# Windowed attention and FFN in one stream: softmax sums and PSUM copies from VectorE to ScalarE, six raw pairs for eight, a later weight decode

## The chip, the cores and the metric

The kernel runs on one core of one Trainium2 chip. The core has five engines that matter here: TensorE (PE, matmuls; its weight loads are listed as PEld), VectorE (DVE), ScalarE (ACT), GpSimd (POOL), and SyncE (SP), which only issues DMAs. Each works through its own list of instructions in order and waits on semaphores of the others. The metric is the device time of one execution in microseconds (us), the median of several runs.

## The reference

Attention over 8 batches and 8 heads of width 64, with 512 local tokens and 32 global ones, and then a two-layer FFN over all 4352 tokens that come out of it.

```python
s_g = scale * np.matmul(q_g, k_all.transpose(0, 1, 3, 2))      # global queries see everything
out_g = np.matmul(sm(s_g), v_all)
mask = np.abs(pos[:, None] - pos[None, :]) <= window            # window = 32
s_ll = np.where(mask, s_ll, -1000000000.0)                      # local queries see a band ...
s_l = np.concatenate([s_lg, s_ll], axis=-1)                     # ... and the 32 global keys
out_l = np.matmul(sm(s_l), np.concatenate([v_g, v_l], axis=2))
...
h = x @ w_in                                                    # x: 4352 x 512, w_in: 512 x 2048
g = np.maximum(h, 0.0) + alpha * np.minimum(h, 0.0)
return (g @ w_out).astype(np.float32)
```

`sm` is a softmax whose sum has 1e-9 added before the division.

## The kernel before

**Units.** The main loop counts units u. FFN unit t = u - 19 is one block of 128 hidden columns (of 16) for one group of tokens: `f1(t)` does twelve 128x512 matmuls into the PSUM tile `h_ps` (three for each of four input blocks, since x and the weights are split into a high and a low part), then VectorE makes `g` from it in two steps (L404, L405), ScalarE rounds it to `gh` (L407) and GpSimd takes the rest, `gl` (L408). `f2(t)` does twelve matmuls from `gh` and `gl` into four output banks, two units later (`LAG`). There are nine groups: one of 512 tokens for each batch, and one of the 256 global tokens. Units 0 to 18 (`NPRE` = 19) have attention alone.

**Attention.** A pair P is two heads of one batch; there are 32, four to a batch and so to a group. Pair P is worked on in units 4P to 4P+3 and finishes in the next two or three. In each unit a score block is made (`local_scores`, two row blocks of 128 queries): matmuls into `s_ps`, on VectorE one custom step for each row block that adds the mask, scales and finds the extreme (L243), on ScalarE the exponential with its row sum z (L247). Then `softmax_tail`: VectorE adds 1e-9 to the two sums one by one (L208) and takes the reciprocal (L209), ScalarE multiplies the rows (L214). The probabilities are transposed into `pt_sb` and multiplied with v into `o_ps`.

**Raw pairs and others.** The first `NRAW` pairs take q and k as they are in float32 (`qk_raw`, loaded whole by `load_pair`). Their probabilities are transposed on TensorE into PSUM (`transpose_pe`, `global_transposes`), copied to `pt_sb` by the engines that the strings `PEC` and `PEG` name for the pair's two heads ("a" ScalarE, "d" VectorE; L302 and L304), and in part by VectorE's 32-wide transposes (L318, L291). The other pairs have q and k rounded by ScalarE and split by GpSimd (`prep_qk`, tiles `hi` and `kl`, L189, L192, L195), and their probabilities go through one large VectorE transpose (L324) and a DRAM scratch, the global ones through 16 small VectorE transposes (L297).

**Weights.** 32 pieces (f, j), 512 KB each, come as 64-bit words (tile `wraw`) and are decoded once: two ScalarE steps (L112, L113), three VectorE steps, which are a clamp (L114), a shift (L116) and a merge (L117), a GpSimd addition (L119); a unit later ScalarE rounds (L125) and GpSimd takes the rest (L126). `weights_step(u)` runs at the end of each unit; `RATE` gives the pieces for units before and from 19, and each piece's load is issued six pieces ahead. Six loads are issued ahead of the loop. `f1(t)` needs piece 2t, `f2(t)` piece 2t+1.

**Order.** A scheduler orders each engine's list from priorities and a model of durations; `boost` gives attention a higher priority. From unit `PIN` on, TensorE's list keeps the program's order. In units below `NWARM` = 18, `WARM` = (2, 2) adds two matmuls of zeros ahead of the attention work and two behind it.

**Group change.** `split_x` rounds a finished batch's attention output to `xh` (ScalarE, L386) and takes the rest as `xl` (VectorE, L387), four blocks for a group, in the unit ahead of the group's first.

Of the kernel before, what the change touches and what calls it, by code (L numbers as in the profile page):

```python
# [8 lines left out]
F32 = mybir.dt.float32  # L9
# [3 lines left out]
AF = mybir.ActivationFunctionType  # L13
ALU = mybir.AluOpType
# [6 lines left out]
NC = DM // 128  # L21
NQ, NK = 512, 640
NEG = -8.0e9
NKR = 704
PEC = "ad"
PEG = "da"
NWARM = 18
WARM = (2, 2)
NRAW = 8
NWB = 33  # L30
NST = 18
NNP = [(0, 0), (0, 2)]
# [27 lines left out]
def longformer_ffn(ctx: ExitStack, tc: tile.TileContext, qk, qkr, gn, vt, vx, w, alpha, out):  # L60
    nc = tc.nc
# [35 lines left out]
    def stage(name, dtype=F32):  # L97
        return work.tile([128, 512], dtype, tag="st", name=name, bufs=NST)
# [23 lines left out]
    def split_weights(f, j):  # L122
        t = wmid.pop((f, j))
        wt = wpool.tile([128, 2, 512], F32R, tag="w", name="wt")
        nc.scalar.copy(wt[:, 0, :], t)  # L125
        nc.gpsimd.tensor_tensor(wt[:, 1, :], t, wt[:, 0, :].bitcast(F32), op=ALU.subtract)  # L126
        wts[f, j] = wt
# [41 lines left out]
    def load_v(P):  # L169
# [27 lines left out]
    def s_bank(P, kind):  # L197
        tag = BT[kind] if P < NPAIR else "s"
        return psum.tile([128, 512], F32, tag=tag, name=kind + "_ps", bufs=2 if tag in "hs" else 1)

    def small(name, n=2):
        return work.tile([128, n], F32, tag=name, name=name, bufs=3)

    def softmax_tail(ranges, z, n, pool=False):
        parts = 128
        rz = small("rz")
        for e in range(n):
            nc.vector.tensor_scalar(rz[:parts, e : e + 1], z[:parts, e : e + 1], 1e-9, None, op0=ALU.add)  # L208
        nc.vector.reciprocal(rz[:parts, 0:n], rz[:parts, 0:n])  # L209
        for e, r in enumerate(ranges):  # L210
            if pool:
                nc.gpsimd.tensor_scalar(r, r, rz[:parts, e : e + 1], 1.0, op0=ALU.mult, op1=ALU.mult)
            else:
                nc.scalar.activation(r, r, AF.Copy, scale=rz[:parts, e : e + 1])  # L214

    def local_scores(P, h, a, pool=False):
# [4 lines left out]
        for e in range(2):  # L221
            i = 2 * a + e
            if P < NRAW:
                n, c0 = 160, 0
# [6 lines left out]
            else:  # L231
# [4 lines left out]
                masks.append(mask[:, c0 : c0 + n])  # L236
            if P < NRAW:
                ranges.append(p_sb[:, base : base + n])
            else:
                ranges.append(sub_ap(p_sb, 0, 128, 896 * h + 4 * c0 + 32 * i, ((128, n // 32), (1, 32))))  # L240
        for e, pr in enumerate(ranges):
# [4 lines left out]
            )  # L246
            nc.scalar.activation(pr, pr, AF.Exp, bias=mn[:, e : e + 1], scale=-1.0, accum_out=z[:, e : e + 1])  # L247
# [34 lines left out]
    def global_transposes(P):  # L282
        if P < NRAW:
            ps = pt_bank(P, 2).rearrange("p (e q) -> p e q", e=4)
            for e in range(2):
                nc.tensor.transpose(ps[:, e, :], sg_sb[:, 128 * e : 128 * e + 128], ident)
            for h in range(2):
                copy(PEG[h], sub_ap(pt_sb, 0, 128, h * 1280 + 64, ((320, 2), (640, 2), (1, 32))), sub_ap(ps, 0, 128, 32 * h, ((128, 2), (64, 2), (1, 32))))
        for h in range(2):
            if P < NRAW:  # L290
                nc.vector.transpose(pt_sb[32:64, h, 3, 1, 64:96], sg_sb[32 * h : 32 * h + 32, 256:288])  # L291
                continue
            for a in range(2):
                for j in range(4):
                    src = sub_ap(sg_sb, 64 * a + 32 * h, 32, 32 * j, ((128, 2), (1, 32)))
                    dst = sub_ap(pt_sb, 32 * j, 32, 640 * h + 512 + a * 64, ((32, 2), (1, 32)))
                    nc.vector.transpose(dst, src)  # L297
            nc.vector.transpose(sub_ap(pt_sb, 32, 32, 1280 + 640 * h + 512 + 96, ((1, 32),)), sg_sb[32 * h : 32 * h + 32, 256:288])

    def copy(engine, dst, src):  # L300
        if engine == "a":
            nc.scalar.copy(dst, src)  # L302
        else:
            nc.vector.tensor_copy(dst, src)  # L304
# [76 lines left out]
    def split_x(G, c):  # L381
        kind, b = GROUPS[G]
        n = SL if kind == "l" else NB * SG
        src = (x_raw if kind == "l" else x_glb)[:, c, 0:n]
        xh, xl = stage("xh", F32R), stage("xl", F32R)
        nc.scalar.copy(xh[:, 0:n], src)  # L386
        nc.vector.tensor_tensor(xl[:, 0:n], src, xh[:, 0:n].bitcast(F32), op=ALU.subtract)  # L387
# [50 lines left out]
    def live(P):  # L438
        return 0 <= P < NPR
# [89 lines left out]
    pieces = [(f, j) for f in range(NF) for j in range(2)]  # L529
    ahead = 6  # L530
    state = [0]

    def weights_step(u):
        k = state[0]
        n = RATE[0][u % len(RATE[0])] if u < NPRE else RATE[1][u % len(RATE[1])]
        new = [i for i in range(k, min(k + n, len(pieces)))]
        for i in new:
            if i + ahead < len(pieces):
                load_weights(*pieces[i + ahead])
            decode_words(*pieces[i])  # L540
# [9 lines left out]
        return tc.high_priority(offset=HP) if u >= HPU else nullcontext()  # L550

    load_pair(0)
    for k in range(ahead):
        load_weights(*pieces[k])
    NT = len(GROUPS) * NF
    for t in range(-NPRE, NT + LAG):
        u = t + NPRE
        pinned[0] = u >= PIN
        if u < NWARM:
# [3 lines left out]
        G, f = divmod(t + 1, NF)  # L563
# [93 lines left out]
```

## Time and profile before

| | us |
|---|---|
| median of 3 timed runs (1019.73 to 1021.2) | 1019.75 |
| the profiled execution | 1017.19 |
| its span, first to last instruction | 1015.4 |

| engine busy over the span | us | share |
|---|---|---|
| TensorE | 984.7 | 97% |
| VectorE | 659.9 | 65% |
| ScalarE | 507.4 | 50% |
| GpSimd | 407.7 | 40% |

The profile is of one execution. Its page gives totals by engine, then the span in 40 equal slices with one digit for each slice (9 is 90% busy or more). A group row has line, engine, operation, out<-in with shapes, xcount, then busy us, mean ns of one, and idle us before it with what ended that wait. A timeline row has start, length, engine, line, operation and in brackets the idle time before it. Busy time counts overlapped instructions of an engine once, so that a busy sum is a little less than count times mean. TensorE's weight loads run beside its matmuls.

### The profile page before, as it was taken

How to read it: one execution, taken by the hardware profiler on the slowest of the kernel's cores; microseconds unless marked ns; L12 is line 12 of the kernel's file. 1: busy time of each engine (PE TensorE's matmuls, PEld its weight loads, DVE VectorE, ACT ScalarE, POOL GpSimd, SP SyncE). 2: the span in 40 equal slices, each digit the busy share in tenths (PEclk: the TensorE clock that was granted, in tenths of full speed). 3: DMA queues.
4: the chain of work that ended last, by engine and by line, in shares of the span. 5: the costliest groups of instructions: out<-in, count | busy, mean ns of one | idle time of the engine just before them, and what ended most of it. 6: DMA issues, size and time to landing. Idle time of an engine off the chain costs nothing.

```text
span 1015.4 us, 17227 instructions
## 1 busy us (share of the span) xinstructions
PE 984.7 (97%) x5592; PEld 790.2 (78%) x5592; DVE 659.9 (65%) x2274; ACT 507.4 (50%) x1347; POOL 407.7 (40%) x330
## 2 busy tenths in 40 slices
PE   7798989998999999999999999999999999999998
PEld 4455767776888888888888888888888888888798
DVE  8978778776666766676767666766667665322322
ACT  6667566575445555455446555654555542211121
POOL 7611567653344344334344344433443432222222
PEclk9987999999999999999999999999999999999999
DMA  9545432145444554455455554455455532100010
GB/s 349 224 141 176 140 116 68 60 123 185 147 138 133 177 158 137 141 167 169 135 152 158 171 153 143 144 179 157 118 149 178 159 107 79 42 1 1 1 43 22
DMA packets 95275, 133.01 MB, mean 131 GB/s; under 512 B 10192, under 2 KB 53712, under 8 KB 95184
## 3 DMA queue, kind: packets, MB, share of 16 engines
q1 hardware_dynamic: 95184, 131.91, 41.5%
q8 instruction: 44, 0.72, 0.3%
q14 instruction: 47, 0.39, 0.1%
HBM read 100.93 MB, written 30.93 MB: 130 GB/s over the span
## 4 chain that ended last, share of the span: by engine, by line
PE 84%; DVE 9%; ACT 2%; issue 2%; DMA 1%; POOL 0%; SPq 0%; DVEq 0%; ACTq 0%; POOLq 0%
PE o L92 35%; PE h_ps L92 35%; PE o_ps L92 5%; PE s_ps L92 5%; PE g_ps L92 3%; DVE wt L114 1%; DVE wt L117 1%; DVE pt_sb L318 1%; DVE p_sb L243 1%; PE warm L92 1%; ACT p_sb L214 1%; DVE g L404 1%; DVE wt L116 1%; DVE g L405 1%; ACT p_sb L247 0%
## 5 line engine op out<-in xcount | busy, mean ns | idle before, releaser
L92 PE MATMUL h_ps<-xh,wt 128*128 128x512 f32 (+1 forms) x1152 | 351.8, 389 | 2.8 <-DVE g L405 2.8
L408 POOL TENSOR_TENSOR gl<-g,gh 128x512 fp32r<-128x512 f32 (+1 forms) x144 | 177.5, 1233 | 418.1 <-ACT gh L407 382.6
L92 PE MATMUL o<-gh,wt 128*128 128x512 f32 (+1 forms) x1152 | 282.5, 386 | 1.5 <-ACT ost L302 1.5
L92 PEld LDWEIGHTS o<-gh,wt 128*128 128x128 f32 x1152 | 205.8, 188 | 48.5 <-ACT ost L302 2.5
L92 PEld LDWEIGHTS h_ps<-xh,wt 128*128 128x128 f32 x1152 | 207.4, 191 | 43.4 <-DVE g L405 3.3
L92 PE MATMUL h_ps<-xl,wt 128*128 128x512 f32 (+1 forms) x576 | 222.4, 387 | 0.9 <-DVE xl L387 0.9
L407 ACT CAST gh<-g 128x512 fp32r<-128x512 f32 (+1 forms) x144 | 86.1, 598 | 260.9 <-DVE g L405 241.4
L404 DVE TENSOR_SCALAR g<-h_ps,alpha_sb 128x512 f32<-128x512 f32 (+1 forms) x144 | 103.3, 717 | 125.3 <-PE h_ps L92 123.0
L214 ACT ACTIVATE p_sb<-p_sb,rz 128x192 f32<-128x192 f32 (+1 forms) x252 | 102.3, 454 | 118.1 <-DVE rz L209 115.8
L92 PE MATMUL o<-gl,wt 128*128 128x512 f32 (+1 forms) x576 | 151.4, 383 | 0.0
L247 ACT ACTIVATE p_sb<-p_sb,mn 128x224 f32<-128x224 f32 (+2 forms) x256 | 115.8, 454 | 39.5 <-DVE mn L243 39.3
L92 PEld LDWEIGHTS h_ps<-xl,wt 128*128 128x128 f32 x576 | 109.4, 190 | 25.2 <-DVE xl L387 1.1
L92 PEld LDWEIGHTS o<-gl,wt 128*128 128x128 f32 x576 | 104.5, 188 | 23.9 <-issue 0.8
L208 DVE TENSOR_SCALAR rz<-z 128x1 f32<-128x1 f32 x256 | 38.3, 151 | 97.4 <-ACT p_sb L247 96.0
L297 DVE STREAM_TRANSPOSE pt_sb<-sg_sb 32x64 f32<-32x64 f32 x384 | 90.6, 236 | 10.6 <-ACT sg_sb L280 4.9
L192 POOL TENSOR_TENSOR hi<-rawq,hi 64x512 fp32r<-64x512 f32 x48 | 62.1, 1294 | 88.0 <-DMA vt<-in_vt_dram 50.1
L405 DVE SCALAR_TENSOR_TENSOR g<-h_ps,g 128x512 f32<-128x512 f32 (+1 forms) x144 | 94.1, 653 | 2.8
L195 POOL TENSOR_TENSOR kl<-rawk,hi 128x640 fp32r<-128x640 f32 x48 | 75.9, 1582 | 3.8
L119 POOL TENSOR_TENSOR wt<-wt,wr 128x512 int32<-128x512 int32 x32 | 42.4, 1324 | 77.2 <-DVE rz L208 40.2
L243 DVE CUSTOM_DVE_ANT_0 p_sb<-s_ps,mask 128x192 f32<-128x192 f32 x192 | 64.3, 364 | 13.5 <-PE s_ps L92 11.9
L92 PE MATMUL o_ps<-pt_sb,vt 128*64 128x160 f32 (+4 forms) x832 | 68.2, 288 | 3.6 <-ACT pt_sb L302 1.7
L92 PEld LDWEIGHTS o_ps<-pt_sb,vt 128*64 128x64 f32 (+2 forms) x832 | 48.7, 135 | 21.9 <-issue 11.9
(85 smaller groups left out, 1043.7 us busy)
## 6 DMA issues: line engine op xcount, KB each, us to landing
scratch<-p_sb SPq DMA_DIRECT2D x192, 112.0 KB, 2.4
wraw<-in_w_dram SPq DMA_DIRECT2D x32, 512.0 KB, 6.7
vt<-in_vt_dram SPq DMA_DIRECT2D x32, 512.0 KB, 4.9
rawk<-in_qk_dram SPq DMA_DIRECT2D x96, 160.0 KB, 2.9
rawq<-in_qk_dram SPq DMA_DIRECT2D x96, 128.0 KB, 2.7
pt_sb<-scratch SPq DMA_DIRECT2D x48, 256.0 KB, 2.8
gn<-in_gn_dram SPq DMA_DIRECT2D x32, 304.0 KB, 5.3
pt_sb<-scratch SPq DMA_DIRECT2D x48, 192.0 KB, 2.9
```

The costliest lines, as they stand in the source:

```text
L92: ins = nc.tensor.matmul(*a, **k)
L119: nc.gpsimd.tensor_tensor(ti, ti, r, op=ALU.add)
L192: nc.gpsimd.tensor_tensor(q, raw[64:128], q.bitcast(F32), op=ALU.subtract)
L195: nc.gpsimd.tensor_tensor(kl[P, h], raw, t.bitcast(F32), op=ALU.subtract)
L214: nc.scalar.activation(r, r, AF.Copy, scale=rz[:parts, e : e + 1])
L243: nc.vector.tensor_tensor_reduce(out=pr, in0=s[:, 256 * e : 256 * e + nn], in1=masks[e], scale=-0.125, scalar=3.0e38, op0=ALU.add, op1=ALU ...
L247: nc.scalar.activation(pr, pr, AF.Exp, bias=mn[:, e : e + 1], scale=-1.0, accum_out=z[:, e : e + 1])
L297: nc.vector.transpose(dst, src)
L404: nc.vector.tensor_scalar(g[:, 0:n], h[:, 0:n], 0.0, alpha_sb[:, f : f + 1], op0=ALU.min, op1=ALU.mult)
L405: nc.vector.scalar_tensor_tensor(g[:, 0:n], h[:, 0:n], 0.0, g[:, 0:n], op0=ALU.max, op1=ALU.add)
L407: nc.scalar.copy(gh[:, 0:n], g[:, 0:n])
L408: nc.gpsimd.tensor_tensor(gl[:, 0:n], g[:, 0:n], gh[:, 0:n].bitcast(F32), op=ALU.subtract)
```

## The change

The edits: the sum z + 1e-9 becomes one ScalarE instruction for both sums; `PEC` and `PEG` name ScalarE alone; `NRAW` is 6 for 8; for group 0 three of the four `xl` go to GpSimd; the first six weight loads are issued one in each of units 0 to 5, inside `weights_step`; no piece is decoded before unit 3 (`WFIRST`), then one in every second unit up to unit 18, then two in each unit; `PIN` is 28 for 36. `NWARM` and `WARM` stay as they are. Lines below line 29 or so move by one or two.

```diff
-PEC = "ad"
-PEG = "da"
+PEC = "aa"
+PEG = "aa"
 NWARM = 18
 WARM = (2, 2)
-NRAW = 8
+NRAW = 6
...
-PIN = 36
+PIN = 28
...
-RATE = ((1, 1, 0), (2, 1))
+WFIRST = 3
+RATE = ((0, 1), (2,))
...
         rz = small("rz")
-        for e in range(n):
-            nc.vector.tensor_scalar(rz[:parts, e : e + 1], z[:parts, e : e + 1], 1e-9, None, op0=ALU.add)
+        nc.scalar.activation(rz[:parts, 0:n], z[:parts, 0:n], AF.Copy, bias=1e-9)
         nc.vector.reciprocal(rz[:parts, 0:n], rz[:parts, 0:n])
...
         nc.scalar.copy(xh[:, 0:n], src)
-        nc.vector.tensor_tensor(xl[:, 0:n], src, xh[:, 0:n].bitcast(F32), op=ALU.subtract)
+        eng = nc.gpsimd if G == 0 and c < NC - 1 else nc.vector
+        eng.tensor_tensor(xl[:, 0:n], src, xh[:, 0:n].bitcast(F32), op=ALU.subtract)
         xs[G, c] = (xh, xl)
...
     def weights_step(u):
+        if u < ahead:
+            load_weights(*pieces[u])
         k = state[0]
         n = RATE[0][u % len(RATE[0])] if u < NPRE else RATE[1][u % len(RATE[1])]
+        n = n if u >= WFIRST else 0
...
     load_pair(0)
-    for k in range(ahead):
-        load_weights(*pieces[k])
     NT = len(GROUPS) * NF
```

The scheduler makes new lists of it. ScalarE's list begins before with four decode steps of two pieces, then the first exponentials:

```order
L112 ACT_TABLE_LOAD
L112 ACTIVATE wt<-wraw 128x512
L113 ACTIVATE wr<-wraw 128x512
L112 ACTIVATE wt<-wraw 128x512
L113 ACTIVATE wr<-wraw 128x512
L247 ACTIVATE p_sb,z<-p_sb,mn 128x160 x4
L112 ACTIVATE wt<-wraw 128x512
L113 ACTIVATE wr<-wraw 128x512
```

Now the same place reads so:

```order
L247 ACT_TABLE_LOAD
L247 ACTIVATE p_sb,z<-p_sb,mn 128x160 x4
L208 ACTIVATE rz<-z 128x2
L113 ACTIVATE wt<-wraw 128x512
L114 ACTIVATE wr<-wraw 128x512
L208 ACTIVATE rz<-z 128x2
L113 ACTIVATE wt<-wraw 128x512
L114 ACTIVATE wr<-wraw 128x512
```

The exponentials (L247) stand first, the new sums (L208) are among them, and the first decode steps, now L113 and L114, come behind.

The second place is VectorE's list between the last steps of FFN units 8 and 9, before:

```order
L243 ISA p_sb,mn<-s_ps,rmask 128x160
L243 ISA mn 128x1
L243 ISA p_sb,mn<-s_ps,rmask 128x160
L243 ISA mn 128x1
L114 TENSOR_SCALAR wt<-wt 128x512
L208 TENSOR_SCALAR rz<-z 128x1
L116 TENSOR_SCALAR wt<-wt 128x512
L208 TENSOR_SCALAR rz<-z 128x1
L404 TENSOR_SCALAR g<-h_ps,alpha_sb 128x512
L117 SCALAR_TENSOR_TENSOR wt<-wraw,wt 128x512
L209 RECIPROCAL rz<-rz 128x2
L405 SCALAR_TENSOR_TENSOR g<-h_ps,g 128x512
```

And now, up to the same step (L406 there), behind the small transposes of the pair before:

```order
L243 ISA p_sb,mn<-s_ps,mask 128x6x32
L243 ISA mn 128x1
L115 TENSOR_SCALAR wt<-wt 128x512
L117 TENSOR_SCALAR wt<-wt 128x512
L115 TENSOR_SCALAR wt<-wt 128x512
L118 SCALAR_TENSOR_TENSOR wt<-wraw,wt 128x512
L117 TENSOR_SCALAR wt<-wt 128x512
L118 SCALAR_TENSOR_TENSOR wt<-wraw,wt 128x512
L405 TENSOR_SCALAR g<-h_ps,alpha_sb 128x512
L209 RECIPROCAL rz<-rz 128x2
L406 SCALAR_TENSOR_TENSOR g<-h_ps,g 128x512
```

Two pieces stand ahead of the unit's g for one, the two sums are gone, and the scores are those of a pair that is not raw (`mask` for `rmask`).

The third place is TensorE's list inside FFN unit 16, the first of group 1, before (pair 7, raw, finishes amid the unit's matmuls):

```order
L92 MATMUL h_ps<-xh,wt 128x512 x2
L92 MATMUL o_ps<-pt_sb,vt 64x96 x2
L92 MATMUL o_ps<-pt_sb,vx 64x64 x2
L92 MATMUL o_ps<-pt_sb,vt 64x2x64 x2
L92 MATMUL o_ps<-pt_sb,vt 64x96 x2
L92 MATMUL o_ps<-pt_sb,vx 64x64 x2
L92 MATMUL o_ps<-pt_sb,vt 64x2x64 x2
L92 MATMUL h_ps<-xl,wt 128x512
```

And now the unit and the scores ahead of it:

```order
L93 MATMUL s_ps<-hi 128x224
L93 MATMUL s_ps<-kl,hi 128x224
L93 MATMUL s_ps<-hi 128x192
L93 MATMUL s_ps<-kl,hi 128x192
L93 MATMUL h_ps<-xh,wt 128x512 x2
L93 MATMUL h_ps<-xl,wt 128x512
```

The unit's twelve matmuls now follow one another, as in all later units of both lists; this holds from FFN unit 9 on, and before from unit 18 on. From the last matmul of FFN unit 20 on, TensorE's list is the same in both.

## The prediction

> **What bounds the kernel now.** I read the page's totals and slices first, then a table of windows, then single rows. In the totals TensorE (PE) is busy 97% of the span; no other engine is above 65%.
>
> ```profile
> PE 984.7 (97%) x5592; PEld 790.2 (78%) x5592; DVE 659.9 (65%) x2274; ACT 507.4 (50%) x1347; POOL 407.7 (40%) x330
> PE   7798989998999999999999999999999999999998
> DVE  8978778776666766676767666766667665322322
> ```
>
> The average hides two regimes. In the first ten slices (254 us) VectorE (DVE) is at 6 to 9 tenths; behind them TensorE is full. To cut the trace into stretches I use VectorE's last step of FFN unit t, called g(t): g(0), g(12), g(20) are these three instructions.
>
> ```profile
> 96.74 0.69 DVE L405 SCALAR_TENSOR_TENSOR g<-h_ps,g 128x512 f32<-128x512 f32 x1
> 196.26 0.67 DVE L405 SCALAR_TENSOR_TENSOR g<-h_ps,g 128x512 f32<-128x512 f32 x1
> 259.95 0.65 DVE L405 SCALAR_TENSOR_TENSOR g<-h_ps,g 128x512 f32<-128x512 f32 x1
> 0.00:97.40 97.40, 81.11 (x536) 50.94 (x536) 79.51 (x306) 67.34 (x196) 43.41 (x50) 0.91 0.63 227
> 97.40:196.90 99.50, 95.14 (x547) 71.00 (x548) 78.85 (x208) 61.35 (x147) 63.92 (x50) 0.94 0.30 102
> 196.90:260.60 63.70, 58.86 (x334) 46.58 (x333) 45.82 (x167) 37.24 (x98) 28.43 (x23) 0.97 0.44 134
> 260.60:1015.40 754.80, 749.63 (x4178) 621.70 (x4176) 455.73 (x1599) 341.50 (x906) 271.92 (x208) 1.00 0.41 122
> ```
>
> The last four rows give window, length, then busy time (instructions) of PE, its weight loads, DVE, ACT, POOL, then granted clock, DMA share, GB/s. In the **prelude**, to g(0), TensorE's 81 us hold 72 warming matmuls; the busiest engine with work to do is VectorE, 79.5/97.4 = 82%. In the **ramp**, g(0) to g(12), TensorE is busy 96% at clock 0.94, VectorE 79%. In the **settling** stretch, g(12) to g(20), eight units take 63.7 us. The last 754.8 us are TensorE at 99%, in a rhythm:
>
> ```profile
> 274.68 2.13 PE L92 MATMUL o<-gh,wt 128*128 128x512 f32 x8
> 301.67 2.13 PE L92 MATMUL o<-gh,wt 128*128 128x512 f32 x8
> ```
>
> Those two rows are the same place of two successive pairs: 27.0 us for four units, 6.75 a unit.
>
> **The end: no change.** In the order, TensorE's 3776 instructions from the last matmul of unit 20 on are the same before and after. TensorE is busy there 749.6 of 754.8 us, so VectorE's and ScalarE's edits lie beneath it; cover lost would show only if VectorE, now 456 of 755, became the slower one. I keep 754.8. The whole question is when g(20) comes: 260.6 now.
>
> **Prelude.** The order puts g(0) behind the same attention work in both (42 score blocks, 5.25 pairs) but less else.
>
> ```profile
> L117 DVE SCALAR_TENSOR_TENSOR wt<-wraw,wt 128x512 uint32<-128x512 uint32 x13 | 12.5, 964 | 0.1
> L116 DVE TENSOR_SCALAR wt<-wt 128x512 uint32<-128x512 uint32 x13 | 10.0, 766 | 0.1
> L114 DVE TENSOR_SCALAR wt<-wt 128x512 f32<-128x512 f32 x13 | 9.2, 706 | 0.8 <-ACT wt L112 0.7
> L318 DVE STREAM_TRANSPOSE pt_sb<-p_sb 32x128 f32<-32x128 f32 x30 | 9.0, 299 | 2.1 <-PE o_ps L92 1.7
> L208 DVE TENSOR_SCALAR rz<-z 128x1 f32<-128x1 f32 x42 | 5.8, 146 | 1.0 <-ACT p_sb L247 0.7
> L304 DVE COPY pt_sb<-pt 128x512 f32<-128x512 f32 (+1 forms) x9 | 4.6, 508 | 1.9 <-PE pt L286 1.9
> L387 DVE TENSOR_TENSOR xl<-x_raw,xh 128x512 fp32r<-128x512 f32 x4 | 3.0, 744 | 0.0
> ```
>
> VectorE loses five of 13 pieces (31.7/13 = 2.44 us each, 12.2), all 42 sums (5.8), eight copies (one of the nine stands behind g(0): 3.9), three xl (2.2) and three transposes that slip behind g(0) (0.9): 25.0. It keeps 54.5 us. ScalarE now has the longer list. Its rows:
>
> ```profile
> L113 ACT ACTIVATE wr<-wraw 128x512 int32<-128x512 uint32 x13 | 8.7, 672 | 0.0
> L112 ACT ACTIVATE wt<-wraw 128x512 f32<-128x512 f32 x13 | 8.7, 672 | 4.4 <-DMA wraw<-in_w_dram 4.4
> L125 ACT CAST wt<-wt 128x512 fp32r<-128x512 f32 x13 | 8.0, 615 | 1.0 <-POOL wt L119 1.0
> L302 ACT COPY pt_sb<-pt 128x512 f32<-128x512 f32 x8 | 4.7, 582 | 0.2 <-PE o_ps L92 0.2
> L302 ACT COPY pt_sb<-pt 128x128 f32<-128x128 f32 x8 | 2.0, 255 | 2.2 <-DVE pt_sb L304 2.2
> L247 ACT ACTIVATION_READ_ACCUMULATOR p_sb<-p_sb,mn 128x1 f32 x256 | 48.8, 190 | 0.0
> L189 ACT CAST hi<-rawk 128x640 fp32r<-128x640 f32 x48 | 34.9, 727 | 0.0
> L189 ACT CAST hi<-rawq 128x512 fp32r<-128x512 f32 x48 | 29.7, 619 | 24.7 <-issue 13.7 <-PE s_ps L92 11.0
> ```
>
> It loses five pieces (25.4/13 = 1.95 each, 9.8) and gains four large copies (2.3), six small ones (1.5), two casts of pair 6 (1.3) and 21 small sums. No row shows ScalarE at 128x2: the ends are 0 (it cannot give time back) and 0.255, the 128x128 copy. I take 0.19, the 128x1 read, which is nearer in size: 4.0. Together 67.3 - 9.8 + 9.1 = 66.6 us. If the busiest engine again fills 82% of the time, 66.6/0.82 = **81 us**, I take 82, for 97.4. The bounds are 76 (a share of 0.88, below) and 97 (a chain of waits between ScalarE and VectorE that the relief doesn't shorten). The new sum on ScalarE waits only for ScalarE's own exponentials; behind it stand the next exponentials, and the reciprocal on VectorE waits for it, one short hop in place of 0.3 us of VectorE. Three xl of some 1.3 us go to GpSimd (POOL), as for the gl row below, whose 43.4 us fall by five pieces at the same time; that is covered.
>
> The loads of the first six pieces leave the head of the SyncE queue, where they stood ahead of the global keys and the second pair.
>
> ```profile
> 5.11 2.40 PE L92 MATMUL s_ps<-qk_raw 64*64 64x160 f32 x16 [5.11 <-DMA qk_raw<-in_qkr_dram]
> ACT p_sb L247 <- DVE mn L243: 12.1, 13, 3.0
> ```
>
> I cost that at nothing: the first scores wait 5.11 us for the first pair's data, which was ahead of the pieces already and is what is late next; the 4.4 us that ScalarE waited for a piece (row L112) lie beside it. The second row is of the waits of this stretch: ScalarE stood 12.1 us, 13 times, for VectorE's scores; the second rival comes back to it.
>
> **Ramp.** Here the work comes back. The order has 24 pieces between g(0) and g(12) where 18 stood, and attention reaches 8.4 pairs for 7.75, the last of them in the other form (pair 6 on).
>
> ```profile
> L117 DVE SCALAR_TENSOR_TENSOR wt<-wraw,wt 128x512 uint32<-128x512 uint32 x18 | 15.5, 863 | 0.3
> L116 DVE TENSOR_SCALAR wt<-wt 128x512 uint32<-128x512 uint32 x18 | 14.8, 824 | 0.2
> L114 DVE TENSOR_SCALAR wt<-wt 128x512 f32<-128x512 f32 x18 | 13.0, 724 | 8.6 <-ACT wt L112 8.3 <-issue 0.2
> L297 DVE STREAM_TRANSPOSE pt_sb<-sg_sb 32x64 f32<-32x64 f32 x384 | 90.6, 236 | 10.6 <-ACT sg_sb L280 4.9
> L324 DVE STREAM_TRANSPOSE p_sb<-p_sb 128x896 f32<-128x896 f32 x48 | 52.9, 1102 | 5.8 <-ACT p_sb L214 5.8
> L243 DVE CUSTOM_DVE_ANT_0 p_sb<-s_ps,mask 128x224 f32<-128x224 f32 x96 | 36.8, 383 | 8.4 <-PE s_ps L92 8.4
> 20.00:40.00 20.00, 15.14 (x59) 9.72 (x58) 17.64 (x48) 12.17 (x32) 14.39 (x12) 0.91 0.78 298
> ```
>
> VectorE gains 12 clamps and shifts and five merges (12 x 0.77 + 5 x 0.86 = 13.6), 32 small transposes (7.6), four large ones (4.4) and 19 scores of at most 0.38 for 14 of 0.32 (2.5); it loses 20 sums (2.9), six copies (2.9) and six transposes (1.8). That is +20.5: 78.9 becomes 99.4, call it 100 us. TensorE needs no more than now, and at the steady rhythm 12 x 6.75 = 81; so VectorE sets the pace. At which share is not in the trace: it reached 79% while TensorE was the bound, and 17.64/20 = 88% in its fullest slice of those I cut, the last row. The ends are 0.82 (122 us) and TensorE's own 0.96 (104). I take 0.88: **114 us**, for 99.5.
>
> Behind each clamp on VectorE stands the unit's g, which the second FFN matmuls wait for; so a piece that comes late, now twice in a unit, holds TensorE too.
>
> **Settling.** From unit 9 on (before: 18) TensorE's order after is the steady one, and pair 7 no longer needs the raw form. Eight units at 6.75 are **54 us**, for 63.7; VectorE's list there falls from 45.8 to some 37. If the ramp leaves a backlog it is up to 60.
>
> **Sum.** 82 + 114 + 54 = 250, against 260.6: 10.6 us less. The span of 1015.4 becomes 1004.8, the profiled execution 1017.19 becomes 1006.6; on the scale of the timed runs (median 1019.75, 2.6 above the profiled one) it is **1009**.
>
> [...] VectorE's pieces stand beside GpSimd's:
>
> ```profile
> 8.17 0.42 DVE L116 TENSOR_SCALAR wt<-wt 128x512 uint32<-128x512 uint32 x1
> 125.41 1.43 DVE L116 TENSOR_SCALAR wt<-wt 128x512 uint32<-128x512 uint32 x1
> 125.27 1.29 POOL L119 TENSOR_TENSOR wt<-wt,wr 128x512 int32<-128x512 int32 x1 [1.70 <-DVE wt L117]
> L408 POOL TENSOR_TENSOR gl<-g,gh 128x512 fp32r<-128x512 f32 (+1 forms) x144 | 177.5, 1233 | 418.1 <-ACT gh L407 382.6
> ```
>
> The shift took 0.42 us with no GpSimd instruction beside it, 1.43 when one had begun just before. [...] GpSimd's list in the ramp grows from 63.9 to some 88 us (nine more half-pieces, nine prepared keys and queries), 64% to 77%. Yet a piece cost 2.44 us in the prelude with GpSimd at 45% and 43.3/18 = 2.41 in the ramp at 64%: the price has not followed the share, so the sum keeps it.
>
> **Rivals.**
> - *Pieces blocked* (slower): each of the 24 pieces is blocked once more than now, 1.43 - 0.42 = 1.0 us. VectorE has 124 us in the ramp, 141 at 0.88; 82 + 141 + 54 = 277, so 1036. It decides from 0.4 us a piece, where the ramp is 124.6 and the gain gone. For it: the pair of rows; against it: 2.44 and 2.41.
> - *Prelude bound by the chain* (slower): g(0) stays at 97, 97 + 114 + 54 = 265, so 1024. For it: the 12.1 us that ScalarE waited for VectorE's scores; against it: VectorE at 82%, so that those waits were mostly for a busy engine.
> - *Work only moved*: the ramp at 0.82 is 122; 258 in all, 1017, no change to speak of.
> - *Better packing*: prelude at 0.88 (76), ramp at 0.96 (104): 234, so 993.
> - Of the words on the change, the warm rows are in neither file's difference: 72 warming matmuls in both orders. They give nothing.
>
> **Chances.** Forecast 0.46 (its own range 1002 to 1016), better packing 0.20, work only moved 0.13, blocked 0.12, chain 0.09. A measurement of this kernel tells 0.2%, 2 us, from no change. So faster 0.66, same 0.13, slower 0.21. The range for 8 in 10 leaves out most of "blocked" and the far end of "better packing": 991 to 1024.
>
> **What would show it.** g(0) near 82, g(12) near 196, g(20) near 250, and from there 755 us with the rhythm of 27.0. VectorE's list of 54 us ahead of g(0) and 100 in the ramp checks the count; its busy share in the ramp (0.88) checks the step I am least sure of; the mean of the three decode rows there (2.41) decides the first rival. Wrong would be a g(0) above 90, or eight settling units above 60.

## The result and the profile after

The changed kernel takes 1027.39 us (median of 7 runs, 1025.96 to 1032.98); the kernel before took 1017.06 in the runs beside it. The ratio is 1.0111, with a 95% interval of 1.0076 to 1.0145: **slower by 1.1%**, where 1% less was forecast. The profiled execution took 1026.28 us, its span 1024.5, against 1017.19 and 1015.4 before. Ratios leave out executions over 1.5% above the fastest of their kernel, which are three of ten of one kernel below (b2) and none of the others.

The page of the changed kernel, engines and slices as before:

```profile
PE 977.4 (95%) x5508; PEld 788.6 (77%) x5508; DVE 641.2 (63%) x2021; ACT 534.7 (52%) x1491; POOL 425.5 (42%) x341
PE   7898787879999999999999999999999999999998
DVE  7847989866666666676666666766667665322322
```

VectorE was relieved: 641 us for 660. In slices 5 to 8 it is nevertheless at 8 to 9 tenths, where it was at 7 to 8, and TensorE has dips there. The same three cuts, the ends of VectorE's last step of units 0, 12 and 20 (now line L406), in the view of windows (length; busy time and count of PE, weight loads, DVE, ACT, POOL; granted clock, DMA share, GB/s):

```profile
0.00:91.50 91.50, 78.87 (x538) 49.81 (x540) 60.38 (x234) 64.36 (x213) 36.55 (x45) 0.94 0.62 216
91.50:212.40 120.90, 94.08 (x510) 72.77 (x506) 109.98 (x249) 81.89 (x204) 91.55 (x69) 0.90 0.45 137
212.40:268.70 56.30, 54.21 (x287) 43.79 (x288) 36.10 (x119) 30.53 (x83) 26.02 (x20) 0.95 0.51 154
268.70:1024.50 755.80, 750.21 (x4179) 622.25 (x4177) 434.77 (x1422) 357.90 (x994) 271.43 (x208) 1.00 0.40 122
```

| stretch | before | forecast | after |
|---|---|---|---|
| prelude, to g(0) | 97.4 | 82 | 91.5 |
| ramp, g(0) to g(12) | 99.5 | 114 | 120.9 |
| settling, g(12) to g(20) | 63.7 | 54 | 56.3 |
| rest | 754.8 | 754.8 | 755.8 |
| span | 1015.4 | 1004.8 | 1024.5 |

The signs are those of the forecast, and every size is worse: 9.5, 6.9, 2.3 and 1.0 us, 19.7 in all. The ramp has eaten what prelude and settling gave (5.9 + 7.4) and 8 us more. TensorE's busy time in the ramp hardly changed (95.1 us before, 94.1 after); its idle time went from 4.4 to 26.8 us. Most of that idle time ends with a VectorE step. The longest of these waits in the changed kernel, in the view of waits (who waited for whom: us in total, times, longest):

```profile
PE h_ps L93 <- DVE g L406: 12.0, 3, 7.4
PE pt L313 <- DVE mn L243: 3.5, 1, 3.5
```

So VectorE's in-order list is what TensorE meets there, whether it is late because it is long or because its steps take longer.

What became dearer in the ramp stands in VectorE's groups (count, busy us, mean ns). Changed kernel, then the kernel before, in its own ramp:

```profile
L118 DVE SCALAR_TENSOR_TENSOR wt<-wraw,wt 128x512 uint32<-128x512 uint32 x23 | 23.5, 1021 | 0.3
L117 DVE TENSOR_SCALAR wt<-wt 128x512 uint32<-128x512 uint32 x24 | 19.9, 829 | 0.4
L115 DVE TENSOR_SCALAR wt<-wt 128x512 f32<-128x512 f32 x24 | 19.3, 802 | 2.9 <-ACT wt L113 2.7
L277 DVE SCALAR_TENSOR_TENSOR gz<-gz 64x1 f32<-64x1 f32 x3 | 3.4, 1134 | 0.0
```

```profile
L277 DVE SCALAR_TENSOR_TENSOR gz<-gz 64x1 f32<-64x1 f32 x2 | 0.3, 149 | 0.0
```

A piece costs 1.021 + 0.829 + 0.802 = 2.65 us for 2.41, and a step on a 64x1 tile costs 1134 ns for 149: it has next to no data, so most of that microsecond is not work. Single rows of the changed kernel show what stands beside such steps, first VectorE's, then GpSimd's (start, length):

```profile
141.95 1.41 DVE L117 TENSOR_SCALAR wt<-wt 128x512 uint32<-128x512 uint32 x1
143.39 1.66 DVE L118 SCALAR_TENSOR_TENSOR wt<-wraw,wt 128x512 uint32<-128x512 uint32 x1
144.97 0.41 DVE L115 TENSOR_SCALAR wt<-wt 128x512 f32<-128x512 f32 x1
145.42 1.38 DVE L117 TENSOR_SCALAR wt<-wt 128x512 uint32<-128x512 uint32 x1
```

```profile
138.47 1.90 POOL L196 TENSOR_TENSOR kl<-rawk,hi 128x640 fp32r<-128x640 f32 x1
141.58 1.49 POOL L409 TENSOR_TENSOR gl<-g,gh 128x512 fp32r<-128x512 f32 x1
143.03 1.47 POOL L127 TENSOR_TENSOR wt<-wt 128x512 fp32r<-128x512 f32 x1
145.22 1.29 POOL L120 TENSOR_TENSOR wt<-wt,wr 128x512 int32<-128x512 int32 x1 [0.72 <-DVE wt L118]
```

The shift of 141.95 ends at 143.36, 0.29 us behind GpSimd's 143.07; that of 145.42 ends at 146.80, 0.29 behind 146.51. The clamp at 144.97, begun with GpSimd idle, takes 0.41. Of the 71 decode steps of this ramp, the 21 with no GpSimd instruction beside them took 0.41 to 0.43 us (clamps and shifts) or 0.67 to 0.69 (merges). 36 took longer, each of them beside a GpSimd instruction: 26 clamps and shifts ended 0.28 or 0.29 us behind the end of one, ten merges 0.55 us. Of the other 14, which had one beside them too, 13 took the short times and one, a shift, 0.82 us. In the ramp before, 23 of 54 ended so behind a GpSimd instruction. The three 64x1 steps of the changed kernel each end within 0.02 us of a GpSimd instruction's end; the two of before, at 149 ns, had none beside them. GpSimd's own rows are longer too: L127 took 1413 ns in the ramp of the changed kernel, where the same subtraction, L126 before, took 1305 in its ramp.

```profile
L127 POOL TENSOR_TENSOR wt<-wt 128x512 fp32r<-128x512 f32 x22 | 31.1, 1413 | 0.8 <-ACT wt L126 0.6
```

```profile
L126 POOL TENSOR_TENSOR wt<-wt 128x512 fp32r<-128x512 f32 x18 | 23.4, 1305 | 8.6 <-ACT wt L125 4.3 <-issue 3.9
```

This suggests another account of the ramp: GpSimd's instructions and VectorE's three decode steps as one resource. I merged the intervals of both groups in the ramp's rows: they cover 85.9 of 99.5 us before (86%) and 111.9 of 120.9 after (93%). VectorE's whole list covers 110.0, or 91%. The two accounts lie close; the experiments f2, e4, g2 and g3 were made to tell them apart.

### The profile page after: what moved, and what is told of

Same layout as the page of the kernel before. It is cut to its first block, busy times and chain, and to the rows that moved or that the text cites. A ratio compares the mean times of both kernels' runs of the same rounds, so it can differ in the third digit from the quotient of the medians.

```text
span 1024.5 us, 16876 instructions
## 1 busy us (share of the span) xinstructions
PE 977.4 (95%) x5508; PEld 788.6 (77%) x5508; DVE 641.2 (63%) x2021; ACT 534.7 (52%) x1491; POOL 425.5 (42%) x341
## 4 chain that ended last, share of the span: by engine, by line
PE 84%; DVE 9%; ACT 3%; DMA 2%; issue 2%; POOL 0%; SPq 0%; DVEq 0%; ACTq 0%
PE h_ps L93 34%; PE o L93 33%; PE o_ps L93 6%; PE s_ps L93 5%; PE g_ps L93 3%; PE warm L93 2%; DVE wt L118 2%; DVE wt L115 1%; DVE wt L117 1%; DVE pt_sb L297 1%; ACT p_sb L214 1%; DVE g L405 1%; DVE p_sb L243 1%; DMA rawk<-in_qk_dram 1%; ACT p_sb L247 1%
## 5 line engine op out<-in xcount | busy, mean ns | idle before, releaser
L405 DVE TENSOR_SCALAR g<-h_ps,alpha_sb 128x512 f32<-128x512 f32 (+1 forms) x144 | 103.2, 717 | 137.0 <-PE h_ps L93 135.8
L214 ACT ACTIVATE p_sb<-p_sb,rz 128x192 f32<-128x192 f32 (+1 forms) x252 | 102.5, 454 | 79.4 <-DVE rz L209 75.4
L247 ACT ACTIVATE p_sb<-p_sb,mn 128x224 f32<-128x224 f32 (+2 forms) x256 | 115.8, 454 | 51.6 <-DVE mn L243 51.5
L93 PEld LDWEIGHTS o<-gl,wt 128*128 128x128 f32 x576 | 104.4, 188 | 23.5 <-issue 0.2
L297 DVE STREAM_TRANSPOSE pt_sb<-sg_sb 32x64 f32<-32x64 f32 x416 | 98.1, 236 | 27.7 <-ACT sg_sb L280 21.9
L193 POOL TENSOR_TENSOR hi<-rawq,hi 64x512 fp32r<-64x512 f32 x52 | 67.7, 1301 | 98.7 <-DMA vt<-in_vt_dram 43.7
L406 DVE SCALAR_TENSOR_TENSOR g<-h_ps,g 128x512 f32<-128x512 f32 (+1 forms) x144 | 94.0, 653 | 2.9
L243 DVE CUSTOM_DVE_ANT_0 p_sb<-s_ps,mask 128x192 f32<-128x192 f32 x208 | 70.6, 369 | 27.9 <-PE s_ps L93 27.0
L196 POOL TENSOR_TENSOR kl<-rawk,hi 128x640 fp32r<-128x640 f32 x52 | 82.3, 1583 | 9.2 <-ACT hi L190 5.6
L93 PE MATMUL o_ps<-pt_sb,vt 128*64 128x160 f32 (+4 forms) x816 | 65.3, 289 | 3.2 <-DVE mn L243 1.9
L209 DVE RECIPROCAL rz<-rz 128x2 f32<-128x2 f32 x128 | 20.9, 163 | 75.7 <-ACT rz L208 74.4
L324 DVE STREAM_TRANSPOSE p_sb<-p_sb 128x896 f32<-128x896 f32 x52 | 57.4, 1104 | 7.9 <-ACT p_sb L214 7.7
```

Source lines behind the costliest of these rows:

```text
L93: ins = nc.tensor.matmul(*a, **k)
L193: nc.gpsimd.tensor_tensor(q, raw[64:128], q.bitcast(F32), op=ALU.subtract)
L196: nc.gpsimd.tensor_tensor(kl[P, h], raw, t.bitcast(F32), op=ALU.subtract)
L243: nc.vector.tensor_tensor_reduce(out=pr, in0=s[:, 256 * e : 256 * e + nn], in1=masks[e], scale=-0.125, scalar=3.0e38, op0=ALU.add, op1=ALU ...
L324: nc.vector.transpose(pr, pr)
L405: nc.vector.tensor_scalar(g[:, 0:n], h[:, 0:n], 0.0, alpha_sb[:, f : f + 1], op0=ALU.min, op1=ALU.mult)
```

## The experiments

All ratios are to the kernel before, run on the same chip in turn. The scheduler makes new lists for every kernel, so a part of a difference can come from the lists; and each row below is of one execution, while the executions of one kernel lie up to 7 us apart for the changed kernel and up to 12 for the others (17 for b2). A difference of a few microseconds between two rows is therefore weak evidence by itself. The rows are of the view of windows again.

### The prelude: fewer and more warming matmuls

```diff
-WARM = (2, 2)
+WARM = (1, 1)      # e3
+WARM = (3, 3)      # e6
```

> The changed kernel with one warming matmul ahead and one behind for two and two (36 for 72). Theory 'warm list': the chain of the prelude has 24.9% of 95 us in warming matmuls, so g(0) comes up to 11 us earlier, about 82, and the total about 1017. Rival 'ScalarE and VectorE chain': warming matmuls only fill idle time, g(0) stays within 2 us of 91.5, total 1026. Rival 'clock': the granted clock of the prelude falls below 0.94 and takes the gain back or more: 1026 to 1035.

> The changed kernel with three warming matmuls ahead and three behind (108 for 72). Theory 'clock': with two fewer the granted clock of the prelude fell from 0.94 to 0.78 and g(0) came 7 us later; with two more it stays at 0.94 or above, and g(0) is at 88 to 92, total 1020 to 1027. Theory 'list': 36 more of 0.23 us on TensorE's path, g(0) 8 us later, about 99, total 1034.

e3 took 1033.79 us, ratio 1.0157 [1.0116, 1.0197]; e6 took 1028.88, 1.0124 [1.0093, 1.0155]. Preludes of e3, then e6:

```profile
0.00:98.30 98.30, 84.11 (x503) 52.39 (x505) 61.83 (x238) 65.70 (x216) 36.88 (x45) 0.78 0.59 208
```

```profile
0.00:97.30 97.30, 87.25 (x566) 54.90 (x566) 62.63 (x238) 65.17 (x216) 36.55 (x45) 0.95 0.62 216
```

VectorE and ScalarE have the same work as in the changed kernel (62 and 65 us), and yet g(0) comes 6.8 us later with 36 matmuls fewer and 5.8 later with 36 more. In e3 the granted clock falls from 0.94 to 0.78, and TensorE is busy 5 us longer with fewer instructions; in e6 the clock holds and the list is longer. Both ways of moving g(0) go through TensorE. The clock rival held for e3. For e6, g(0) fits the list (97.3 for an expected 99), but the total lies between the two expectations, only 1.5 us above the changed kernel's: its ramp and settling are 3.4 us shorter (119.3 and 54.5). The chain of ScalarE and VectorE, by which g(0) would have stayed, fell.

The chain of waits says the same of the changed kernel's prelude, by line:

```profile
by line: PE warm L93 25.9%; PE s_ps L93 16.9%; PE o_ps L93 15.3%; PE g_ps L93 5.4%; DMA qk_raw<-in_qkr_dram 4.8%; PE pt L313 4.4%; ACT p_sb L247 3.9%; DVE pt_sb L318 2.8%; PE h_ps L93 2.5%; ACT p_sb L214 2.0%; POOL p_sb L212 1.9%; PE pt L28
```

The same view before:

```profile
by line: PE o_ps L92 10.3%; PE s_ps L92 10.3%; issue 8.9%; PE warm L92 8.1%; DVE pt_sb L318 6.2%; DVE wt L114 5.9%; DVE wt L117 5.3%; DMA wraw<-in_w_dram 4.9%; DVE p_sb L243 4.8%; DMA qk_raw<-in_qkr_dram 4.0%; PE h_ps L92 3.4%; ACT p_sb L21
```

Warming matmuls are a quarter of it, for 8% before, when the chain went through VectorE's decode steps, scores and transposes as well. VectorE is not out of it, though. Two windows of the changed kernel:

```profile
20.00:40.00 20.00, 15.83 (x98) 9.86 (x97) 19.30 (x48) 16.37 (x48) 15.42 (x13) 1.00 0.80 305
60.00:80.00 20.00, 20.00 (x162) 12.89 (x160) 11.17 (x58) 15.51 (x57) 2.57 (x2) 1.00 0.38 130
```

From 20 to 40 us VectorE is nearly full and TensorE waits; from 60 to 80 TensorE is full. That fits e4 (below), where less GpSimd work, with the same warming matmuls, brought g(0) to 86.8. How an idle gap adds to that, in TensorE's rows and two windows of the changed kernel:

```profile
34.80 2.39 PE L93 MATMUL warm<-idle 128*128 128x512 f32 x8
40.06 1.10 PE L93 MATMUL s_ps<-qk_raw 64*64 64x160 f32 x8 [2.88 <-DVE x_glb L354]
41.09 0.79 PE L93 MATMUL warm<-idle 128*128 128x512 f32 x1
```

```profile
30.00:40.00 10.00, 7.18 (x62) 4.49 (x60) 9.67 (x25) 8.32 (x23) 7.27 (x6) 1.00 0.56 204
40.00:50.00 10.00, 9.94 (x42) 5.88 (x43) 5.99 (x31) 5.65 (x24) 4.99 (x4) 0.52 0.75 238
```

TensorE stood 2.88 us for a VectorE step that came behind two decode steps, and then the clock was at half for 10 us (0.52 in the second window; a warming matmul took 0.79 us there, 0.40 at 36.79), in which VectorE was busy only 60% of the time. Five half-clock stretches stand in the changed kernel's trace from there to g(20), of 3.4, 6.8 and 10.2 us. What brings one on, and how long a gap it takes, was not tried apart.

g(0) moved with the clock without a change of the warming, too. Among the kernels with the relief and 72 warming matmuls (e2, b2 and e1 are below), g(0) comes at 91.5 us with a granted clock of 0.94, at 96.3 with 0.87 (e2), at 105.5 with 0.80 (b2) and at 109.2 with 0.78 (e1). TensorE's idle time in these preludes is 11 to 14 us throughout; what grows is its busy time.

### Each part of the change alone

b1 has the later decode and the spread first loads on the kernel before, b2 the relief (sums and copies to ScalarE, three xl to GpSimd), b3 the pairs:

```diff
-NRAW = 8
+NRAW = 6
-PIN = 36
+PIN = 28
```

> The kernel before with the later decode and the spread first loads alone. Theory 'blocked': the pieces moved from the prelude into the ramp stand there beside more GpSimd work, their price rises from 2.41 to 2.6 us and the ramp grows by more than the prelude shrinks: g(0) 97.4 to about 90, ramp 99.5 to about 117, total +8 to +12. Rival 'relief is what costs' (the move of sums and copies to ScalarE): this kernel stays within 3 us of the one before.

> The kernel before with the relief of VectorE alone (sums and PSUM copies on ScalarE, three xl on GpSimd). Theory 'TensorE at half clock sets the prelude': VectorE loses 12 us of its prelude, but g(0) moves only if the granted clock does not fall: at 0.91 some 92, at 0.8 some 105; the ramp shrinks by up to 5 us. Rival 'VectorE sets the prelude': g(0) at 85, total -12.

> The kernel before with six raw pairs and the list kept from unit 28 alone. By the counts VectorE gains 12 us in ramp and settling and TensorE loses 8: if VectorE sets the ramp, ramp 99.5 to 108 or more and settling 63.7 to 56: within 3 us of before. If TensorE sets it (busy 96% there), -8.

b1: 1018.69, ratio 1.0022 [1.0007, 1.0036]. b2: 1022.01, 1.0020 [0.9992, 1.0048]. b3: 1019.27, 1.0036 [1.0014, 1.0058]. Prelude and ramp of b1:

```profile
0.00:89.40 89.40, 80.38 (x536) 50.60 (x536) 66.49 (x290) 58.83 (x182) 29.11 (x40) 0.92 0.63 227
89.40:201.60 112.20, 98.31 (x569) 71.46 (x568) 98.63 (x239) 72.69 (x172) 79.35 (x59) 0.94 0.31 107
```

Prelude of b2, then ramp of b3:

```profile
0.00:105.50 105.50, 91.30 (x538) 56.72 (x540) 73.21 (x253) 72.65 (x228) 46.69 (x53) 0.80 0.59 211
```

```profile
98.50:197.90 99.40, 88.80 (x489) 68.77 (x490) 89.15 (x224) 66.94 (x160) 77.55 (x59) 0.94 0.46 148
```

Of b1 the mechanism came as expected: prelude -8, ramp +12.7, and a price of 2.60 us a piece (1.011 + 0.848 + 0.745, the means of its ramp) for an expected 2.6. The sum was smaller, +2.5 us and not +8, which by the total alone is what its rival said. Its prelude is shorter than the changed kernel's, although VectorE has 6 us more in it, so there is no sign that the relief bought anything there. b2 met its first theory and not its rival: the relief took 6.3 us from VectorE's prelude (12 were counted), and g(0) came at 105.5, 8 us later, at a clock of 0.80, where 105 at 0.8 was expected. That is the profiled execution of 1023.7 us; the ten spread from 1014.6 to 1031.5, and in this one only the clock of the prelude was low. b3 met neither expectation: VectorE's list in the ramp grew by 10 us and GpSimd's by 14, TensorE's fell, and the length stayed at 99.4 us. The ramp had room for both.

The three parts alone cost 2.2, 2.0 (not told from nothing) and 3.6 thousandths; together 11.1. So the loss is not in one of them. b1 and b3 both lay their work into the same stretch: with b3's 10 and 14 us put on b1's 98.6 and 79.4, VectorE has 109 and GpSimd 93, which is what the kernel with these two parts shows (f1 below: 109.5 and 90.7).

### One part of the change undone

e1 has the rates of before again (the first loads stay spread), e2 eight raw pairs and unit 36, f1 VectorE's sums, copies and xl:

```diff
-WFIRST = 3
-RATE = ((0, 1), (2,))
+WFIRST = 0
+RATE = ((1, 1, 0), (2, 1))     # e1
-PEC = "aa"
-PEG = "aa"
+PEC = "ad"
+PEG = "da"                     # f1, with the sums and xl
```

> The changed kernel with the decode rates of before (RATE = ((1, 1, 0), (2, 1)), no unit skipped at the start). Theory 'warm list': the prelude to g(0), 91.5 us in the changed kernel, is set by TensorE's list with its 72 warming matmuls and not by VectorE (60 of 91.5 us busy), so five more pieces (12 us) fit into VectorE's idle time: g(0) stays at 90 to 94, and the ramp g(0) to g(12) loses six pieces of 2.65 us, 120.9 to about 104: about 1010 us. Theory 'VectorE sets both': g(0) goes back to 97 or later and the ramp gives the same back: 1018 to 1024.

> The changed kernel with eight raw pairs and TensorE's list kept from unit 36, as before. If the extra VectorE work of pairs 6 and 7 (some 12 us of transposes and scores in the ramp) is what makes the ramp long: ramp 121 to about 108, g(12) to g(20) back from 56 to 63, total about 1020. If the ramp is long for the pieces alone (63 of its 110 us of VectorE), the ramp stays at 115 or more, the settling grows to 63: 1030 or more.

> The changed kernel with VectorE's sums, its half of the PSUM copies and its xl given back; later decode, six raw pairs and unit 28 stay. Theory 'VectorE sets the ramp at 0.9 of its busy time': VectorE gets 6 us back there (110 to 116), ramp 121 to about 128; the prelude, set by TensorE, stays at 89 to 92: about 1033. Rival 'the relief itself costs' (a hop to ScalarE in each softmax tail, lower granted clock): 1018 to 1023, with a prelude clock of 0.92 or more.

e1: 1034.10, ratio 1.0139 [1.0077, 1.0201]. e2: 1035.92, 1.0176 [1.0130, 1.0222]. f1: 1029.71, 1.0132 [1.0088, 1.0176]. e1 and e2 in prelude and ramp, then f1 in the ramp:

```profile
0.00:109.20 109.20, 95.39 (x534) 59.34 (x534) 71.51 (x249) 71.36 (x224) 46.23 (x53) 0.78 0.53 191
109.20:216.00 106.80, 91.74 (x487) 70.42 (x488) 90.38 (x202) 70.73 (x178) 78.63 (x59) 0.89 0.45 138
```

```profile
0.00:96.30 96.30, 84.90 (x536) 53.53 (x536) 61.68 (x238) 64.01 (x211) 33.80 (x43) 0.87 0.61 218
96.30:219.00 122.70, 102.55 (x585) 74.12 (x584) 101.33 (x221) 79.77 (x203) 82.36 (x63) 0.92 0.28 96
```

```profile
95.70:220.60 124.90, 99.30 (x510) 75.85 (x506) 109.51 (x271) 78.24 (x183) 90.72 (x68) 0.90 0.41 128
```

e1's ramp went near where the count put it (106.8 for an expected 104). Its prelude of 109.2 and its total fit neither theory: "97 or later" was to come from VectorE, which is busy 72 us of it, while TensorE is busy 95, at a clock of 0.78. e2 met its second branch: without the two pairs' work the ramp is no shorter, its VectorE share is 83%. f1's total, 1029.71, is nearer to the first theory's 1033 than to its rival, but not by the mechanism: VectorE's list in the ramp did not grow to 116 us, it is 109.5 (22 pieces in place of 24), and the prelude of 95.7 is longer than the 89 to 92 expected; the profiled execution took 1032.44. What stayed in all of the long ramps is 24 pieces, or 22 in f1 and b1.

Put side by side, the kernels are nearly all combinations of the three parts:

| parts in the kernel | ratio to before | 95% |
|---|---|---|
| later decode (b1) | 1.0022 | 1.0007 to 1.0036 |
| relief (b2) | 1.0020 | 0.9992 to 1.0048 |
| pairs (b3) | 1.0036 | 1.0014 to 1.0058 |
| later decode and pairs (f1) | 1.0132 | 1.0088 to 1.0176 |
| later decode and relief (e2) | 1.0176 | 1.0130 to 1.0222 |
| relief, pairs, spread loads (e1) | 1.0139 | 1.0077 to 1.0201 |
| all (the changed kernel) | 1.0111 | 1.0076 to 1.0145 |

Any two parts cost more together (1.3 to 1.8%) than their single costs add up to (0.4 to 0.6%), and the third adds nothing that these intervals can tell. This holds for the relief too: beside the pairs and the later decode it changes nothing, but put on the later decode alone (b1 to e2) it costs 1.5%, with a ramp of 122.7 for 112.2 us. So the two pairs are not needed for a long ramp. What the relief does there is not shown; VectorE waits 8.9 us for ScalarE's decode step in e2's ramp, for 4.7 in b1's.

### Who sets the ramp

f2 takes VectorE work away that was not longer beside the busier GpSimd (this step, L405 now and L404 before, took 740 ns in the ramp after, 742 before); f3 does the same to the kernel before. Both also put a ScalarE step ahead of VectorE's. A const tile `beta_sb` holds 1 - alpha:

```diff
-nc.vector.tensor_scalar(g[:, 0:n], h[:, 0:n], 0.0, alpha_sb[:, f : f + 1], op0=ALU.min, op1=ALU.mult)
-nc.vector.scalar_tensor_tensor(g[:, 0:n], h[:, 0:n], 0.0, g[:, 0:n], op0=ALU.max, op1=ALU.add)
+nc.scalar.activation(g[:, 0:n], h[:, 0:n], AF.Relu, scale=beta_sb[:, f : f + 1])
+nc.vector.scalar_tensor_tensor(g[:, 0:n], h[:, 0:n], alpha_sb[:, f : f + 1], g[:, 0:n], op0=ALU.mult, op1=ALU.add)
```

e4 takes GpSimd work away, on the changed kernel:

```diff
-nc.gpsimd.tensor_tensor(ti, ti, r, op=ALU.add)
+nc.gpsimd.tensor_tensor(ti[:, 0:16], ti[:, 0:16], r[:, 0:16], op=ALU.add)
```

g2 (on f2) and g3 (on f3) move a GpSimd step to VectorE:

```diff
-nc.gpsimd.tensor_tensor(gl[:, 0:n], g[:, 0:n], gh[:, 0:n].bitcast(F32), op=ALU.subtract)
+eng = nc.vector if T < 13 else nc.gpsimd
+eng.tensor_tensor(gl[:, 0:n], g[:, 0:n], gh[:, 0:n].bitcast(F32), op=ALU.subtract)
```

> The changed kernel with FFN's nonlinearity as (1 - alpha) relu(h) on ScalarE and one VectorE step (alpha h plus that) in place of two VectorE steps. Theory 'VectorE sets the ramp': 12 steps of 0.74 us go from its 110 us there, ramp 121 to about 111, prelude and settling unchanged: about 1016. Rival 'TensorE's half-clock windows and waits set it': ramp 118 or more, 1024 or more.

> The kernel before with the same single VectorE step. There TensorE set the ramp (busy 96%, VectorE 79%): ramp 99.5 to 96 or more, total within 5 us of before. If VectorE set it, ramp to 89: -10.

> The changed kernel with GpSimd's addition of each decoded piece cut to 16 of 512 columns: the low word's contribution to the other columns of the weights is left out. [...] Rival 'list alone': the price stays 2.6 or more, the ramp 118 or more, total 1024 or more.

> f2 (the changed kernel with one VectorE step per unit) with the gl of units 0 to 12 on VectorE (0.7 us) for GpSimd (1.3 us). Theory 'one resource': joint time of GpSimd and VectorE's conflicting steps falls by some 8 us from 110.6, although VectorE's list grows from 103.5 to 111; the ramp falls from 121.6 to about 113, total about 1020. Rival 'VectorE's list': the ramp grows to 125 or more, 1033 or more.

> f3 (the kernel before with one VectorE step per unit) with the gl of units 0 to 12 on VectorE. Joint time 84.4 of 93.7 us. Theory 'one resource': ramp to 86 to 89, total about 1005. Rival 'VectorE's list' (71 to 79 us) or TensorE (busy 90.4 of 93.7): ramp stays at 92 to 95, about 1010.

f2: 1030.02, ratio 1.0143 [1.0095, 1.0192]. f3: 1010.49, 0.9937 [0.9922, 0.9953]. e4: 1005.17, 0.9874 [0.9824, 0.9924]. g2: 1025.98, 1.0094 [1.0063, 1.0124]. g3: 1015.83, 0.9991 [0.9973, 1.0010]. The ramps, in the order f2, g2, e4, f3, g3:

```profile
90.10:211.70 121.60, 98.12 (x510) 73.85 (x510) 103.53 (x233) 87.30 (x214) 90.29 (x68) 0.92 0.42 132
```

```profile
91.50:208.50 117.00, 96.23 (x510) 73.08 (x510) 107.20 (x224) 87.07 (x208) 78.98 (x57) 0.93 0.45 137
```

```profile
86.80:193.00 106.20, 93.76 (x503) 71.95 (x504) 95.75 (x222) 79.47 (x194) 68.67 (x71) 0.91 0.49 151
```

```profile
97.60:191.30 93.70, 90.41 (x542) 66.89 (x539) 71.10 (x190) 67.33 (x158) 61.06 (x48) 0.98 0.32 106
```

```profile
99.40:194.00 94.60, 90.36 (x541) 67.17 (x538) 80.05 (x209) 68.38 (x160) 48.88 (x37) 0.98 0.31 104
```

| ramp of | length | VectorE | GpSimd | both as one | TensorE idle |
|---|---|---|---|---|---|
| before | 99.5 | 78.9 | 63.9 | 85.9 | 4.4 |
| b3 | 99.4 | 89.2 | 77.6 | 91.4 | 10.6 |
| after | 120.9 | 110.0 | 91.6 | 111.9 | 26.8 |
| e2 | 122.7 | 101.3 | 82.4 | 106.6 | 20.1 |
| f2 | 121.6 | 103.5 | 90.3 | 110.6 | 23.5 |
| g2 | 117.0 | 107.2 | 79.0 | 104.6 | 20.8 |
| e4 | 106.2 | 95.8 | 68.7 | 91.4 | 12.4 |

"Both as one" is the merged time of GpSimd and VectorE's decode steps, in g2 with its gl steps.

f2 is the blow to "VectorE's busy time sets the ramp": 6.5 us less on VectorE, and the ramp is no shorter, as the rival had it; 11.8 of TensorE's 23.5 idle us still end with VectorE's g. e4 is the other half: GpSimd 23 us less, the decode steps unchanged in number, and VectorE is busy 14 us less, the ramp 15 us shorter. Some 5 of the 14 us only moved behind g(12), where VectorE's list grew from 36.1 to 41.5 us. VectorE's groups of e4 in the ramp show where another 6 come from:

```profile
L118 DVE SCALAR_TENSOR_TENSOR wt<-wraw,wt 128x512 uint32<-128x512 uint32 x24 | 22.6, 943 | 0.2
L117 DVE TENSOR_SCALAR wt<-wt 128x512 uint32<-128x512 uint32 x24 | 17.5, 728 | 0.3
L115 DVE TENSOR_SCALAR wt<-wt 128x512 f32<-128x512 f32 x24 | 17.2, 716 | 4.0 <-ACT wt L113 3.9
```

2.39 us a piece for 2.65, as before the change (2.41). With that price, a ramp of 106.2 and a total of 1005.17 the rival "list alone" (2.6 or more, 118 or more, 1024 or more) fell. The total fell by more than the ramp did, since the prelude is 4.7 us shorter too. g2, with VectorE's list 3.7 us longer than f2's and GpSimd's 11.3 shorter, has a ramp 4.6 us shorter. That is the direction of "one resource" and half of the expected size; but 4.6 us between single executions is little, and the intervals of f2's and g2's ratios overlap. "One resource" does not account for all ramps either: it covers 87% of e2's long one and 92% of b3's short one. g3 shows the other regime: GpSimd 12 us less, VectorE 9 more, and the ramp the same 94 us, with TensorE busy 96% at clock 0.98. There TensorE sets it, as it did before the change.

f3 gave more than expected (93.7 us of ramp for "96 or more"): the share of TensorE is the same 96% as before, but the clock in the ramp is 0.98 for 0.94. By the ratios it beats both kernels, by 0.6% and 1.7%; e4 is faster, but leaves part of the decode out.

## Why the prediction was wrong

- **The end** was right: 755.8 us for 754.8, with TensorE busy 750.2 us for 749.6. Settling was right in kind and 2.3 us short of the gain.
- **The prelude** failed at its bound. The step was "TensorE's 81 us hold 72 warming matmuls; the busiest engine with work to do is VectorE". TensorE's share (83%) was as large as VectorE's, and its list was known to stay: 82 us would have left it 1 us of idle time. Warming matmuls are instructions like others: they took 25.9% of the chain of waits in the changed kernel's prelude, the scores 16.9%, and behind the gap of 2.88 us both ran at a clock of 0.52 for 10 us. The count itself was right: the durations of VectorE's instructions there add up to 94.2 us before and 69.2 after, 25.0 less. But overlapped time counts once in the busy time that the 25.0 were taken from, so that it fell by 19.1, to 60.4 and not 54.5. ScalarE's was 64.4 for a counted 66.6, with the small sum at 0.20 us for an assumed 0.19. It did not matter: with TensorE busy 78.9 of 91.5 us, g(0) moved 5.9 and not 15.4. e3 and e6 showed, from both sides, that TensorE sets it from about 40 us on.
- **The ramp** had the right sign and a share that was nearly right (0.91 for 0.88; e2, f1, f2 and g2 have 0.83 to 0.92, so this is in part luck), but the size of VectorE's list was 110.0 and not 99.4. The step was "the price has not followed the share, so the sum keeps it". It rose to 2.65 us a piece (24 x 0.24 = 6 us) and two groups of small steps rose with it (L277 3.0 us, L358 0.9), which is 9.9 of the 10.6 us. The rival "pieces blocked" named this; it set its turning point at 0.4 us a piece, and a price of 0.24 and the small steps reached nearly the same sum. The comparison that spoke against it took an average for the share: GpSimd's 45% of the prelude is 68% of its first 60 us, in which 12 of the 13 pieces were decoded, and nothing from 60 to 90. Over the ramps of all kernels the price does follow the share: 2.03 us a piece with GpSimd busy 52% (g3), 2.37 to 2.44 at 64 or 65% (before, b2, e4, f3), 2.55 to 2.84 at 67 to 78%.
- **The pair of rows** that was weighed, a shift of 0.42 us with no GpSimd instruction beside it and one of 1.43 behind the start of one, agrees with the ramp: half of the decode steps (36 of 71) end a constant time behind a GpSimd instruction, 0.28 us or, for a merge, 0.55. The sum by the trace's mean price was the wrong side to take.
- **The relief** was taken to be worth 12 us of VectorE's prelude and 6 of its ramp. Alone (b2) and as the last part added (f1 to the changed kernel) it has no measurable effect on the total; put on the later decode (b1 to e2) it costs 1.5%.
- **Interaction** was missed altogether: the parts alone cost 0.2 to 0.4%, any two of them together 1.3 to 1.8%.

What stays open: how the 121 us of the long ramp divide between GpSimd with VectorE's decode steps (93% covered) and VectorE's own list (91%). e4 shows that GpSimd's part matters, and f2 that VectorE's busy time alone does not set the length. Neither account explains e2, whose ramp was as long with VectorE at 83% and both as one at 87%. Why the granted clock of e1's, e2's and b2's preludes fell was not tried apart, nor why two parts cost more than their sum; the new list of each kernel may have a share in it.

## What to carry to other kernels

Count an engine's filler work when asking what bounds a stretch: warming matmuls sit in an in-order list, and a list that is full of them is full. Price a moved step by what will run beside it where it goes, not by its mean where it came from, and take an engine's share over the time in which the steps run, not over a stretch with an empty end. Take durations off a sum of durations, and not off a busy time that counts overlaps once. Parts of a change that are nearly free one by one can be dear together, so try them in pairs. And f3, which takes load off VectorE and moves no work in time, gained 0.6% where this change lost 1.1%.

## What the runs showed of the hardware

A VectorE step on a 64x1 tile (L277) took 1134 ns in the mean of three, each with a GpSimd instruction beside it, for 149 ns before, with none. A clamp or a shift of 128x512 took 0.41 to 0.43 us with no GpSimd instruction beside it, and up to 1.5 beside one. GpSimd's instructions were longer too: L127 took 1413 ns in the ramp, for 1305 (as L126) in the ramp before. Half the warming work brought g(0) 7 us later, with the clock at 0.78 for 0.94; half as much again brought it 6 us later at an unchanged clock (0.95). A clock of 0.52 over 10 us followed a gap of TensorE of 2.88 us.
